# Copying two heads' pairs out of PSUM: both copies on ScalarE in place of one on ScalarE and one on VectorE

## The chip, the core and the metric

The kernel runs on one core of a Trainium2 chip. The core has a matrix engine (TensorE, PE in the profile, with its weight loads listed apart as PEld), two engines for elementwise work (VectorE, DVE; ScalarE, ACT), GpSimd (POOL), and a queue on SyncE (SP) that issues the DMA transfers. TensorE writes into PSUM, which VectorE and ScalarE read. The metric is the device time of one execution in microseconds.

## The reference

Attention with a sigmoid in place of the softmax, and behind it a channel mix with a shift by one token. Batch 8, 12 heads, 448 tokens, head size 64; model size 768, hidden size 1024.

```python
scores = scale * np.matmul(q, k.transpose(0, 1, 3, 2)) - np.log(S)
attn = 1.0 / (1.0 + np.exp(-scores))
x = np.matmul(attn, v)                     # heads side by side: (8, 448, 768)

x_prev = np.concatenate([zeros, x[:, :-1, :]], axis=1)
xk = mu_k * x + (1.0 - mu_k) * x_prev
xr = mu_r * x + (1.0 - mu_r) * x_prev
k = np.maximum(xk @ w_k, 0.0)
v = k * k @ w_v
r = 1.0 / (1.0 + np.exp(-(xr @ w_r)))
return r * v
```

## The kernel before, in words

**Attention.** Two heads make a pair; there are N = 48 pairs, and pair n lies with its two heads on partitions 0 to 63 and 64 to 127. The 448 keys of a head are three chunks of 128 (NC = 3) and a tail of 64. The loop (L415) takes two pairs, n and n + 1, per cycle: 24 cycles. TensorE goes through three ways of tiling its array in a cycle:

- `scores` (L324, matmuls L335): six chunks of scores, three for each pair, in tiles of 64 rows by 128 columns. Each chunk is six matmuls (three products of split operands `kh`, `kl`, `qh`, `ql` for two heads) into a buffer `sc[u]` of two PSUM banks. There are four such buffers; after the first cycle the six chunks use u = 1, 2, 3, 0, 1, 2. Behind each chunk ScalarE computes its sigmoid into `pf` (L359), which frees the buffer.
- `weigh` (L362, matmuls L366): six chunks of sigmoids times values, in tiles of 128 by 64, into `av[0]` for the even pair and `av[1]` for the odd one.
- `score_tails` (L340, L344) for the next two pairs and then `weigh_tails` (L369, L374) for these two, in tiles of 64 by 64. The sigmoid of the score tails goes into `pt`.

`av[0]` and `av[1]` are the two banks of the fourth score buffer, `sc[3]` (L197 to L199). So the third chunk of scores of the next cycle (u = 3; the profile lists its matmuls as L335 with output `av`) can start only when both sums have been copied out, and the first `weigh` only when the sigmoid of that chunk has read it.

**Gather.** `gather(n)` (L380) copies `av[n % 2]` into `xx[n % 2]` (the copy is made by `copy_on`, so it stands under L216 in the profile), subtracts the sum shifted by one token (`dx`, L386), and makes two mixes on VectorE, `mr` and `mk` (L389), which SP's queue stores to `xr_d` and `xk_d`. In the kernel before, the copy of an even pair is on ScalarE and that of an odd pair on VectorE.

**What else runs meanwhile.** The weights come in a 64-bit format and VectorE converts them to 32 bits during attention (`convert`, L226); seven combinations of each group of blocks are made for a product scheme with seven multiplications, and those of the router weight `w_r` are split by a cast on ScalarE and a subtraction on VectorE into `slot` (L291, L292). The next pairs' q and k are split in `prepare` (L308): the casts of even pairs on ScalarE, of odd pairs on VectorE.

**The channel mix.** Three stages (R_, K_, V_) of products of 128 by 128 by 448, `multiply` (L564, matmuls L575), each with its operands fetched and split by ScalarE and VectorE.

**The order of the work.** Each operation is entered with `op(engine, cost, prio, ...)`. `Plan.order` (L50) simulates the engines with these costs: a free engine takes, of the operations that are ready, the one with the smallest due time (prio), and a result is ready for another engine 170 ns after its end (WAIT). The program is written in the order of these starts, and each engine then works through its own list in that order; waits come from the tiles that operations share. TensorE's operations are kept in the order in which they are entered. Costs in ns around the change: sigmoid 923, a chunk of scores 591 (plus 184 at the change of tiling), `weigh_tails` 752, the copy on ScalarE `act(S)` = 474, on VectorE `dve(S)` = 602. Due times in cycle n: `prepare` n + 1, `weigh_tails` n + 1.5, the score tails of the next pairs n + 1.7, both gathers n + 1.8, the next cycle's score chunks and sigmoids n + 2 to n + 2.5. The conversions of the weights have due times by a pace of their own.

Of the kernel before, what the change touches and what calls it, by code (L numbers as in the profile page):

```python
# [22 lines left out]
class Plan:  # L23
# [8 lines left out]
    def op(self, engine, cost, prio, run, reads, writes, dma=None):  # L32
        i = len(self.ops)
        deps = set()
        for r in reads:
            if r in self.writer:
                deps.add(self.writer[r])
        for w in writes:
            if w in self.writer:
                deps.add(self.writer[w])  # L40
            deps.update(self.readers.get(w, ()))
        for r in reads:
            self.readers.setdefault(r, []).append(i)
        for w in writes:
            self.writer[w] = i
            self.readers[w] = []
        deps.discard(i)
        self.ops.append(Op(engine, cost, prio, run, deps, dma))
# [50 lines left out]
def attention_then_channel_mix(  # L99
# [15 lines left out]
    nc = tc.nc  # L115
    P = 128
    N, _, S = q.shape
# [81 lines left out]
    av = [sc[3][:, m] for m in range(2)]  # L199

    plan = Plan()
    op = plan.op
    SP, PE, ACT, DVE = "SP", "PE", "ACT", "DVE"
# [5 lines left out]
    def act(n, sbuf=False, ptr=False):  # L209
        return 100 + 0.834 * n + 42 * sbuf + 93 * ptr  # L210

    def dve(n, fast=False, ptr=False):
        return 135 + n / (1.92 if fast else 0.96) + 61 * ptr

    def copy_on(e, dst, src):
        (nc.scalar.copy if e == ACT else nc.vector.tensor_copy)(dst, src)  # L216
# [4 lines left out]
    def dma(dst, src, prio, reads, writes):  # L221
        ns = dst.shape[0] * math.prod(dst.shape[1:]) * 4 / 300
        op(SP, 500, prio, lambda: nc.sync.dma_start(dst, src), reads, writes, dma=ns)  # L223
# [94 lines left out]
    AV = [("sc", 3, h) for h in range(2)]  # L318
# [61 lines left out]
    def gather(n, at):  # L380
        b, j = divmod(n, NP)
        x, d, X, G = xx[n % 2], dx[0], ("xx", n % 2), ("dx", 0)
        cols = slice(b * S, (b + 1) * S)
        e = DVE if n % 2 else ACT
        op(e, act(S) if e == ACT else dve(S), at, lambda: copy_on(e, x[:, 1:], av[n % 2][:, :S]), [AV[n % 2]], [X])
        op(DVE, dve(S), at, lambda: nc.vector.tensor_sub(d, x[:, 1:], x[:, :S]), [X], [G])  # L386
        for name, m, mu, to, stage in (("mr", mr[n % 2], mur, xr_d, R_), ("mk", mk[n % 2], muk, xk_d, K_)):
            M = (name, n % 2)
            op(DVE, dve(S, ptr=True), at, lambda m=m, mu=mu: nc.vector.scalar_tensor_tensor(m, d, mu[:, j:j + 1], x[:, :S], ALU.mult, ALU.add), [X, G, (mu is muk, "mu")], [M])  # L389
            dma(to[j][:, cols], m, at, [M], [("x", stage, j, b)])  # L390
# [24 lines left out]
    for n in range(0, N, 2):  # L415
        early = FILL * (n < 4)
        if n == 0:
            for c, u in enumerate((1, 2, 3)):
                key_chunk(0, c, u, 0)
            prepare(1, -4)  # L420
            last_keys(0, 0.1)
            for c, u in enumerate((1, 2, 0)):
                key_chunk(1, c, u, 0.2)
        else:
            for i, u in enumerate((1, 2, 3, 0, 1, 2)):
                key_chunk(n + i // NC, i % NC, u, n + 0.1 * i)
        for m in (n + 2, n + 3):
            if m < N:
                if m > 2:
                    load(m, n + 0.2 - early)  # L430
                prepare(m, n + 1 - early)
        for m in (n, n + 1):
            for c in range(NC):
                weigh(m, c, n + 1)
        if n + 2 < N:
            last_keys(n + 2, n + 1.7)
        weigh_tails(n, n + 1.5)
        gather(n, n + 1.8)
        gather(n + 1, n + 1.8)
# [19 lines left out]
    e = N % RAW  # L459
# [173 lines left out]
    for stage, w, out7, pace in ((K_, w_k, wk_o, WK_PACE), (V_, w_v, wv_o, WV_PACE)):  # L633
        at = OFF + first[stage - 1]
# [5 lines left out]
    for step, (stage, s, p) in enumerate(steps):  # L640
        at = OFF + step
# [53 lines left out]
```

## Time and profile before

| | before |
|---|---|
| median of 3 runs | 819.69 us (819.4 to 820.19) |
| profiled execution | 818.95 us, of which the span from first to last instruction is 817.2 us |
| granted TensorE clock | 1.000 |
| TensorE matmuls busy | 809.1 us (99%) |
| VectorE busy | 631.5 us (77%) |
| ScalarE busy | 486.9 us (60%) |
| end of attention's last matmuls | 258.3 us from the span's start |

A line of a timeline reads: start in us, duration in us, engine, line, operation, output <- inputs, shapes, count, and in brackets how long the engine stood idle before it and what ended that. In a list of waits the three numbers are microseconds in total, number of times and the longest. In a list of groups they are the busy time in us, the mean in ns of one, and behind the bar the idle time of the engine just before them with what ended it. In the chain in order of time a line reads: start, duration, what. Busy shares are averages over attention and channel mix, which have different limits.

### The profile page before, as it was taken

The page shows a single profiled execution, that of the slowest core. Times are in us where ns is not written, and L with a number is a line of the kernel's source. Part 1 is how long each engine was busy: PE and PEld are TensorE (multiplying, and loading weights), DVE is VectorE, ACT ScalarE, POOL GpSimd, SP SyncE. Part 2 cuts the span into 40 slices and gives each one's busy share as a digit, 9 for nine tenths or more (in the row PEclk, how much of TensorE's full clock was granted, in tenths as well). Part 3 has the DMA queues.
Part 4 walks back from the last instruction along what each step waited for, and adds up shares of the span by engine and source line. Part 5 has one row for each costly group of instructions (what it writes and reads, how often), then busy time and mean ns, then how long its engine had stood idle before and what let it go on. Part 6 is the DMA issues. An engine that isn't in the chain of part 4 may idle for free.

```text
span 817.2 us, 13460 instructions
## 1 busy us (share of the span) xinstructions
PE 809.1 (99%) x4594; PEld 648.8 (79%) x4594; DVE 631.5 (77%) x1184; ACT 486.9 (60%) x833; POOL 0.3 (0%) x6
## 2 busy tenths in 40 slices
PE   8999999999999999999999999999999999999998
PEld 3445455555556999999999999999999999999997
DVE  4989988888889898989898937347497584775944
ACT  5676777777766555556676555656775334343341
POOL 0000000000000000000000000000000000000000
PEclk9999999999999999999999999999999999999999
DMA  7877788788886879576887663523775546655415
GB/s 244 280 238 253 254 253 257 249 277 269 285 290 236 309 226 340 176 274 226 310 241 277 234 205 124 157 92 124 226 224 187 173 155 218 204 180 157 156 47 168
DMA packets 104756, 179.69 MB, mean 220 GB/s; under 512 B 11888, under 2 KB 93296, under 8 KB 104688
## 3 DMA queue, kind: packets, MB, share of 16 engines
q1 hardware_dynamic: 104688, 178.83, 66.5%
q8 instruction: 36, 0.59, 0.3%
q14 instruction: 32, 0.26, 0.1%
HBM read 109.06 MB, written 69.73 MB: 219 GB/s over the span
## 4 chain that ended last, share of the span: by engine, by line
PE 99%; DMA 0%; ACT 0%; issue 0%; DVE 0%; SPq 0%; ACTq 0%
PE pb L575 68%; PE av L366 14%; PE sc L335 10%; PE sc L344 3%; PE av L335 3%; PE av L374 2%; DMA qn<-in_q 0%; PE pb L562 0%; ACT pf L359 0%; DVE pt L606 0%; ACT kh L216 0%; ACT qh L216 0%; SPq L223 0%; ACTq L216 0%
## 5 line engine op out<-in xcount | busy, mean ns | idle before, releaser
L575 PE MATMUL pb<-rr,slot 128*128 128x448 f32 x2076 | 437.1, 362 | 0.0
L575 PEld LDWEIGHTS pb<-rr,slot 128*128 128x128 f32 x2076 | 389.2, 187 | 26.0
L575 PE MATMUL pb<-qh,slot 128*128 128x448 f32 x464 | 151.9, 361 | 0.0
L366 PE MATMUL av<-pf,vn 128*64 128x448 f32 x576 | 113.5, 543 | 0.6 <-ACT pf L359 0.6
L359 ACT ACTIVATE pf<-sc 128x896 f32<-128x896 f32 x120 | 103.6, 940 | 5.5 <-PE sc L335 5.5
L575 PEld LDWEIGHTS pb<-qh,slot 128*128 128x128 f32 x464 | 86.9, 187 | 6.5
L366 PEld LDWEIGHTS av<-pf,vn 128*64 128x64 f32 x576 | 39.2, 137 | 63.7 <-issue 52.9
L575 PE MATMUL pb<-ql,slot 128*128 128x448 f32 x232 | 84.2, 363 | 0.0
L510 ACT CAST rr<-ys 128x448 fp32r<-128x448 f32 x66 | 36.3, 567 | 45.9 <-PE pb L575 45.1
L359 ACT ACTIVATE pt<-sc 128x896 f32<-128x896 f32 x24 | 22.0, 918 | 58.3 <-PE sc L344 58.3
L511 DVE TENSOR_TENSOR rr<-ys,rr 128x448 fp32r<-128x448 f32 x66 | 39.0, 618 | 9.7 <-ACT rr L510 9.6
L335 PE MATMUL sc<-qh,kh 64*128 64x448 f32 x236 | 46.1, 387 | 0.0
L575 PEld LDWEIGHTS pb<-ql,slot 128*128 128x128 f32 x232 | 43.5, 188 | 2.2
L511 DVE TENSOR_TENSOR rr<-pf,rr 128x448 fp32r<-128x448 f32 x38 | 23.2, 623 | 26.4 <-ACT rr L510 26.4
L335 PE MATMUL sc<-ql,kh 64*128 64x448 f32 x236 | 43.0, 361 | 0.0
L335 PE MATMUL sc<-qh,kl 64*128 64x448 f32 x236 | 42.8, 359 | 0.0
L613 ACT COPY pb<-pb 128x448 f32<-128x448 f32 x40 | 20.7, 518 | 32.9 <-PE pb L575 32.9
L617 ACT COPY pf<-pb 128x448 f32<-128x448 f32 x40 | 21.3, 532 | 31.7 <-PE pb L575 28.4
L510 ACT CAST rr<-vn 128x448 fp32r<-128x448 f32 x50 | 27.9, 564 | 19.0 <-PE pb L575 17.6
L335 PEld LDWEIGHTS sc<-qh,kh 64*128 64x128 f32 x236 | 22.1, 184 | 20.1 <-issue 16.9
L511 DVE TENSOR_TENSOR rr<-vn,rr 128x448 fp32r<-128x448 f32 x50 | 29.7, 621 | 6.5 <-ACT rr L510 6.5
L511 DVE TENSOR_TENSOR rr<-qn,rr 128x448 fp32r<-128x448 f32 x28 | 17.4, 621 | 21.7 <-ACT rr L510 21.7
(110 smaller groups left out, 1035.6 us busy)
## 6 DMA issues: line engine op xcount, KB each, us to landing
kn<-in_k SPq DMA_DIRECT2D x48, 224.0 KB, 4.3
qn<-in_q SPq DMA_DIRECT2D x48, 224.0 KB, 4.4
vn<-in_v SPq DMA_DIRECT2D x48, 224.0 KB, 4.5
xr_d<-mr SPq DMA_DIRECT2D x48, 224.0 KB, 4.5
xk_d<-mk SPq DMA_DIRECT2D x48, 224.0 KB, 4.5
pf<-r_d SPq DMA_DIRECT2D x48, 224.0 KB, 3.2
k_d<-pf SPq DMA_DIRECT2D x34, 224.0 KB, 2.1
r_d<-pf SPq DMA_DIRECT2D x28, 224.0 KB, 3.4
```

What stands on the lines that cost most here:

```text
L335: nc.tensor.matmul(sc[u][:, h, :S], kk[half[h], c * P:(c + 1) * P], qq[half[h], :], start=e == 0, stop=e == len(pairs) - 1)
L344: nc.tensor.matmul(sc[u][half[h ^ (m % 2)], m % 2, :S], kn[m % RAW][half[h], KW:], qn[m % RAW][half[h], :], start=True, stop=True)
L359: op(ACT, 923, at, lambda: nc.scalar.activation(f, sc[u][:, :, :S], AF.Sigmoid, bias=NEG_LOG_S, scale=SCALE), R, K)
L366: nc.tensor.matmul(av[n % 2][half[h], :S], vn[n % 5][:, h * NC + c, :], pf[i][:, h, :], start=c == 0, stop=False)
L374: nc.tensor.matmul(av[m % 2][half[r ^ (m % 2)], :S], vn[m % 5][half[r], 2 * NC, :], pt[n // 2 % PTB][half[r], m % 2, :], start=False, stop ...
L510: op(ACT, act(T, True), at, lambda: nc.scalar.copy(hi, y), [Y], [H])
L511: op(DVE, dve(T), at, lambda: nc.vector.tensor_sub(lo, y, hi), [Y, H], [L])
L575: nc.tensor.matmul(b[0], l, r, start=p in (0, 4) and (t, e) == (0, 0), stop=(t, e) == (n - 1, 2), skip_group_check=True)
L613: op(ACT, act(T), at, lambda: nc.scalar.copy(y(), x()), [X], [Y])
L617: op(ACT, act(T), at, lambda: nc.scalar.copy(u, y()), [Y], [U])
```

## The change

Both gathers copy on ScalarE, with the cost `act(S)` in the planner. The copy is now `nc.scalar.copy` in `gather` itself. Since the planner orders the whole program from costs and due times, the order of other operations may differ too.

```diff
         x, d, X, G = xx[n % 2], dx[0], ("xx", n % 2), ("dx", 0)
         cols = slice(b * S, (b + 1) * S)
-        e = DVE if n % 2 else ACT
-        op(e, act(S) if e == ACT else dve(S), at, lambda: copy_on(e, x[:, 1:], av[n % 2][:, :S]), [AV[n % 2]], [X])
+        op(ACT, act(S), at, lambda: nc.scalar.copy(x[:, 1:], av[n % 2][:, :S]), [AV[n % 2]], [X])
         op(DVE, dve(S), at, lambda: nc.vector.tensor_sub(d, x[:, 1:], x[:, :S]), [X], [G])
```

## Prediction

> **What bounds the kernel now.** I read the page first: its busy times and the chain that ended last.
>
> ```profile
> PE 809.1 (99%) x4594; PEld 648.8 (79%) x4594; DVE 631.5 (77%) x1184; ACT 486.9 (60%) x833; POOL 0.3 (0%) x6
> ...
> PE 99%; DMA 0%; ACT 0%; issue 0%; DVE 0%; SPq 0%; ACTq 0%
> PE pb L575 68%; PE av L366 14%; PE sc L335 10%; PE sc L344 3%; PE av L335 3%; PE av L374 2%; DMA qn<-in_q 0%; PE pb L562 0%; ACT pf L359 0%; DVE pt L606 0%; ACT kh L216 0%; ACT qh L216 0%; SPq L223 0%; ACTq L216 0%
> ```
>
> The chain is TensorE from end to end, so a copy out of PSUM matters only where a matmul waits for it. A busy PE hides such waits, because the end of a matmul is modelled; they show at the weight load in front of it. So the next view is the waits, first those of the weight loads between 10 and 258 us, then those of all engines between 20 and 350 us.
>
> ```profile
> PEld av L335 <- DVE xx L216: 4.3, 12, 0.4
> PEld av L335 <- ACT xx L216: 3.9, 11, 0.4
> ```
>
> ```profile
> DVE xx L216 <- ACT xx L216: 13.3, 12, 1.5
> ...
> ACT xx L216 <- DVE xx L216: 6.7, 11, 1.2
> ```
>
> The third score chunk of a cycle is computed into the bank pair `av` (L335 with output av). It waits 12 + 11 = 23 times, once in every cycle that has a successor, 0.36 us each (8.2/23), for whichever copy into `xx` comes second. And the copies do not run side by side, as the planner believes: in 12 cycles VectorE's waits for ScalarE's, in 11 ScalarE's for VectorE's. They take turns. The timeline of one cycle where VectorE goes first:
>
> ```profile
> 154.10 0.93 PE L374 MATMUL av<-pt,vn 64*64 64x448 f32 x8
> ...
> 154.37 0.92 ACT L359 ACTIVATE pt<-sc 128x896 f32<-128x896 f32 x1 [1.44 <-PE sc L344]
> ...
> 155.12 0.62 DVE L216 COPY xx<-av 128x448 f32<-128x448 f32 x1 [0.97 <-PE av L374]
> ...
> 155.84 0.54 ACT L216 COPY xx<-av 128x448 f32<-128x448 f32 x1 [0.55 <-DVE xx L216]
> ...
> 156.07 0.37 PE L335 MATMUL sc<-ql,kh 64*128 64x448 f32 x2
> 156.27 1.73 ACT L359 ACTIVATE pf<-sc 128x896 f32<-128x896 f32 x2
> ...
> 156.42 0.19 PEld L335 LDWEIGHTS av<-qh,kh 64*128 64x128 f32 x2 [0.36 <-ACT xx L216]
> 156.42 0.47 PE L335 MATMUL av<-qh,kh 64*128 64x448 f32 x2
> ...
> 156.73 0.37 PE L335 MATMUL av<-qh,kl 64*128 64x448 f32 x2
> ...
> 157.87 0.94 ACT L359 ACTIVATE pf<-av 128x896 f32<-128x896 f32 x1
> ...
> 158.14 0.19 PEld L335 LDWEIGHTS sc<-qh,kh 64*128 64x128 f32 x2
> ```
>
> The weighted sums end at 155.03 (154.10 + 0.93). VectorE copies until 155.74, ScalarE from 155.84 to 156.38, and TensorE may go on at 156.42. Without a wait, pairs of matmuls follow each other every 0.20 us: 156.07, 156.27, 156.47. The second pair of the waiting chunk starts at 156.73 instead of 156.47, so the wait costs **0.26 us** per cycle, not the 0.36 that the weight load stands idle; the rest is its head start. This 0.26 is the most that any faster copying can win.
>
> The other kind of cycle, ScalarE first, from the timelines of ScalarE, VectorE and the weight loads:
>
> ```profile
> 102.11 0.92 ACT L359 ACTIVATE pt<-sc 128x896 f32<-128x896 f32 x1 [1.69 <-PE sc L344]
> 102.93 0.53 ACT L216 COPY xx<-av 128x448 f32<-128x448 f32 x1
> 103.62 1.73 ACT L359 ACTIVATE pf<-sc 128x896 f32<-128x896 f32 x2 [0.17 <-PE sc L335]
> ```
>
> ```profile
> 103.49 0.62 DVE L216 COPY xx<-av 128x448 f32<-128x448 f32 x1 [1.21 <-ACT xx L216]
> ```
>
> ```profile
> 104.17 0.18 PEld L335 LDWEIGHTS av<-qh,kh 64*128 64x128 f32 x2 [0.36 <-DVE xx L216]
> ```
>
> **The main term: the two copies.** Removed are VectorE's 24 copies and the hand-over between the engines; added are 24 copies on ScalarE.
>
> ```profile
> L216 DVE COPY xx<-av 128x448 f32<-128x448 f32 x24 | 15.0, 626 | 24.0 <-ACT xx L216 13.3 <-PE av L374 10.7
> ...
> L216 ACT COPY xx<-av 128x448 f32<-128x448 f32 x24 | 12.8, 533 | 7.2 <-DVE xx L216 7.2
> ```
>
> When can ScalarE begin? It is busy with the sigmoid of the tails (`pt`). In the second cycle a copy follows that sigmoid's start by 0.82 us (102.11 to 102.93). In the first cycle that is 154.37 + 0.82 = 155.19, a little behind the 155.12 at which VectorE could begin, so the first copy starts 0.07 later than today. How far behind it does the second start? Two copies in a row are nowhere in the trace. The nearest row is a copy followed by another read of PSUM on ScalarE: 155.84 to 156.27, 0.43. The lower bound is 0.41 (a copy followed by a cast out of SBUF, in cycles that carry one), the upper bound 0.54, the copy's whole duration, if two copies do not overlap at all. I take 0.43, the case nearest in operation and memory. Second copy: 155.62 to 156.16, weight load at 156.20 with today's 0.04, second matmul pair 0.31 behind it as today, at 156.51 instead of 156.73: **0.22 us** won of the 0.26. In the other kind of cycle 102.11 + 0.82 + 0.43 + 0.53 + 0.04 = 103.93 against 104.17, 0.24. I take 0.22 for all: 23 x 0.22 = **5.1 us**. With the bounds of the pitch: 0.41 gives 0.24 and 5.5, 0.54 gives 0.11 and 2.5.
>
> [...]
>
> [...]
>
> **The second term: what stands between the copies and the next sigmoid.** Four cycles lose time at another place as well. The chain in order of time, a long cycle and a normal one, and the other three long ones:
>
> ```profile
> 16.54 0.91 PE sc L344 x8
> ...
> 27.58 0.91 PE sc L344 x8
> ...
> 41.91 2.04 PE sc L335 x18
> ...
> 83.77 2.04 PE sc L335 x18
> ...
> 94.40 2.04 PE sc L335 x18
> ...
> 111.51 0.91 PE sc L344 x8
> ...
> 115.45 2.04 PE sc L335 x18
> ...
> 122.15 0.91 PE sc L344 x8
> ...
> 142.96 0.91 PE sc L344 x8
> ...
> 146.90 1.80 PE sc L335 x18
> ...
> 153.36 0.91 PE sc L344 x8
> ```
>
> A normal cycle is 153.36 - 142.96 = 10.40 us, the long one 10.64; its last three chunks take 2.04 instead of 1.80. ScalarE's and the weight loads' timelines say why:
>
> ```profile
> 113.98 0.54 ACT L216 COPY xx<-av 128x448 f32<-128x448 f32 x1 [0.55 <-DVE xx L216]
> 114.41 0.52 ACT L291 CAST slot<-wbits 128x384 fp32r<-128x384 f32 x1
> 114.82 1.73 ACT L359 ACTIVATE pf<-sc 128x896 f32<-128x896 f32 x2
> ```
>
> ```profile
> 116.61 0.18 PEld L335 LDWEIGHTS sc<-qh,kh 64*128 64x128 f32 x2 [0.31 <-ACT pf L359]
> ```
>
> A cast of router weights (0.41 to the next start) sits between copy and sigmoids; the sixth chunk needs the bank that the second sigmoid frees, and waits. The planner put the cast there because it had a hole: counting from the end of the score tails it sees ScalarE free at 170 + 923 + 474 = 1567 ns, but the next sigmoid ready only at 752 + 591 + 184 + 170 = 1697. With a second copy of 474 ScalarE is taken until 2041, the sigmoid is ready by then, and it is due earlier (n + 2) than these casts, which run ahead of their due times. So the cast moves behind the sigmoids, where ScalarE has room (1.44 us idle before `pt` above). 4 x 0.24 = **1.0 us**. If the casts stay, 0; below that the same hole costs 0.24 in cycles that now escape it, which I put into the no-change rival. The first cycle, 27.58 - 16.54 = 11.04, has 0.64 over the normal one; whether the new order mends that I cannot tell, so it goes only into the low end.
>
> **What costs nothing, and why.** The first sigmoid starts behind both copies. In the first cycle above it keeps its 0.43 to the second copy and comes 0.22 earlier with everything behind it; where ScalarE goes first today it comes at 102.93 + 0.86 = 103.79 instead of 103.62. Cover: two sigmoids from 155.62 + 0.43 end at 157.78, and the weight load of the sixth chunk, 158.14 today, would come at 157.92. That leaves 0.14, less 0.04 of signalling 0.10. This is the tightest cover; gone, it costs the 0.24 of the long cycles. VectorE loses 24 copies of 626 ns, which frees nothing that TensorE waits for. Its subtractions now wait for ScalarE's second copy, at 156.16 where today the later copy ends at 156.38 in this cycle; the mixes and SP's stores behind them move the same way. The channel mix has no matmul waiting for these copies, so it starts earlier by the sum and keeps its length.
>
> **Sum.** 5.1 + 1.0 = 6.1 us off the profiled execution's own 818.95 (a span of 817.2 and 1.75 around it): 812.85. The median of the runs is 819.69, 0.74 above that execution: **813.6**.
>
> **The rivals.**
> 1. *The copies do not overlap on ScalarE* (pitch 0.54): 2.5 + 1.0 = 3.5, 816.2. For it: no row of two such copies in a row. Against it: every pair of ScalarE instructions above without a wait between starts before the first has ended (102.11 + 0.92 is 103.03, the copy starts at 102.93).
> 2. *The wait moves to the sixth chunk.* If the first sigmoid is late by more than the cover of 0.10, by a slower pair of copies or by casts that stay behind them, each cycle pays 0.24 there and gains 0.22 before: 23 x 0.02 = 0.5 lost, without the second term, about 820, no change. For it: the cover is thin. Against it: copies and sigmoids shift together, and the order of due times.
> 3. *Casts land in front of the copies* (slower). ScalarE takes its queue in order; a cast between the sigmoid of the tails and the copies delays both by 0.41, so a cycle loses 0.41 - 0.22 = 0.19: in all 23, 4.4 lost, 824. It turns slower than today where the mean delay exceeds 0.22 a cycle. For it: the casts of q and k are due at n + 1, ahead of the copies at n + 1.8, and ScalarE's run of work is one copy longer. Against it: ScalarE stands idle 1.44 and 1.69 us before `pt` in the two cycles above, room for one more copy of 0.43, and no copy above has a cast in front. [...]
>
> **How the numbers follow.** Forecast 0.72, rival 1 0.10, rival 2 0.10, rival 3 0.08. A measurement of this kernel tells about 0.2% (1.6 us) from no change; forecast and rival 1 are faster by more, rival 2 is within, rival 3 slower: 0.82, 0.10, 0.08. The low end takes the whole 0.26 in all cycles (6.0), the 1.0 and the 0.64: 7.6 off, 812.0. The high end reaches past rival 1 to a gain of about 2.5, the first term's bound alone: 817.2. That leaves out rivals 2 and 3.
>
> **What would show it.** Step one: ScalarE's two copies into `xx` 0.41 to 0.45 apart, and the wait of the weight load for `av` at 0.14 us or less in place of 0.36. Step two: no cast between copies and sigmoids, chain pieces of 1.80 throughout, cycles of about 10.18 us, and an attention that ends some 6 us earlier than today's 258. Rival 2 would show weight loads for `sc` waiting for `pf` about 0.3 us in most cycles; rival 3 a cast between `pt` and `xx`. A channel mix whose length changes by over 0.5 us would make the prediction wrong at a place that I did not look for.

## The result, and the profile after

The changed kernel takes **814.51 us** (median of 6 runs, 813.95 to 814.88) where the kernel before takes 819.71 beside it (819.07 to 820.28): a ratio of 0.9936, 95% interval 0.9923 to 0.9949, so 5.2 us or 0.64% less. 813.6 was forecast.

The page after, busy times and the chain by line (in the changed file, the lines behind the edit have a number one smaller, and the copy stands under L384):

```profile
PE 803.4 (99%) x4594; PEld 649.4 (80%) x4594; DVE 619.5 (76%) x1160; ACT 495.5 (61%) x857; POOL 0.3 (0%) x6
...
PE 98%; ACT 1%; DMA 0%; issue 0%; DVE 0%; SPq 0%
```

VectorE has 24 instructions less, ScalarE 24 more, and the chain is still TensorE's. All copies into `xx`, from the view of that tile, and the waits of the weight loads between 10 and 258 us:

```profile
L384 ACT COPY xx<-av x48: 527/539/556, 18.6 to 253.9; 128x448 f32<-128x448 f32 x48
```

```profile
PEld av L335 <- ACT xx L384: 1.0, 1, 1.0
```

Of 23 waits for a copy, 8.2 us in total, one is left, of 1.0 us. A cycle in the timeline:

```profile
140.33 0.93 PE L374 MATMUL av<-pt,vn 64*64 64x448 f32 x8
...
140.60 0.92 ACT L359 ACTIVATE pt<-sc 128x896 f32<-128x896 f32 x1 [2.27 <-PE sc L344]
...
141.41 0.96 ACT L384 COPY xx<-av 128x448 f32<-128x448 f32 x2
...
142.26 1.75 ACT L359 ACTIVATE pf<-sc 128x896 f32<-128x896 f32 x2
142.30 0.37 PE L335 MATMUL sc<-ql,kh 64*128 64x448 f32 x2
...
142.43 0.19 PEld L335 LDWEIGHTS av<-qh,kh 64*128 64x128 f32 x2
...
142.51 0.40 PE L335 MATMUL av<-qh,kh 64*128 64x448 f32 x2
...
142.74 0.37 PE L335 MATMUL av<-qh,kl 64*128 64x448 f32 x2
```

Both copies together take 0.96, with 0.54 for one: the second starts 0.42 behind the first, and the sigmoids 0.85 behind the first. The second matmul pair of the third chunk starts at 142.74, 0.44 behind the last pair of the second chunk; without any wait it would be 0.40. So 0.04 of the 0.26 us is left. The whole attention, in the chain in order of time:

```profile
16.73 0.98 PE sc L344 x8
...
27.61 0.91 PE sc L344 x8
...
231.21 0.91 PE sc L344 x8
...
241.39 0.96 PE sc L344 x8
...
244.20 0.88 ACT xx L384 x2
...
252.47 0.91 PE av L374 x8
253.38 0.81 PE pb L561 x3
...
281.39 527.43 PE pb L574 x2637
```

For comparison the end of the attention of before in the same view:

```profile
246.96 0.91 PE sc L344 x8
...
257.35 0.91 PE av L374 x8
258.26 0.81 PE pb L562 x3
...
286.26 527.42 PE pb L575 x2637
```

Where the time went, interval by interval: the 21 cycles from the second score tails on take 241.39 - 27.61 = 213.78, 10.18 each, where they took 246.96 - 27.58 = 219.38: **-5.60**. The first interval takes 10.88 in place of 11.04: -0.16. The last takes 11.08 in place of 10.39: **+0.69**. That is -5.07 from the first score tails to the first matmul of the channel mix. The channel mix is as long as before (the stretch of 2637 matmuls takes 527.43 and 527.42). The first score tails come 0.19 later in this execution, as the first matmuls do (4.12 against 3.92). In the profiles below these tails start between 15.8 and 17.1 us, so below I compare the stretch from the first score tails to the channel mix ("the attention": 241.72 us before, 236.65 after, each from one profiled execution) beside the medians.

### The profile page after: what moved, and what is told of

Its sections match the earlier page's. It is cut to its first block, busy times and chain, and to the rows that moved or that the text cites. A ratio compares the mean times of both kernels' runs of the same rounds, so it can differ in the third digit from the quotient of the medians.

```text
span 812.3 us, 13502 instructions
## 1 busy us (share of the span) xinstructions
PE 803.4 (99%) x4594; PEld 649.4 (80%) x4594; DVE 619.5 (76%) x1160; ACT 495.5 (61%) x857; POOL 0.3 (0%) x6
## 4 chain that ended last, share of the span: by engine, by line
PE 98%; ACT 1%; DMA 0%; issue 0%; DVE 0%; SPq 0%
PE pb L574 68%; PE av L366 14%; PE sc L335 9%; PE sc L344 3%; PE av L374 2%; PE av L335 2%; DMA qn<-in_q 0%; ACT xx L384 0%; ACT pt L359 0%; ACT pf L359 0%; PE pb L561 0%; DVE pt L605 0%; ACT rr L509 0%; ACT kh L216 0%; ACT qh L216 0%
## 5 line engine op out<-in xcount | busy, mean ns | idle before, releaser
L385 DVE TENSOR_TENSOR dx<-xx 128x448 f32<-128x448 f32 x48 | 29.8, 621 | 18.2 <-ACT xx L384 18.1
```

## The experiments

| kernel | median us | ratio to before (95%) | attention us |
|---|---|---|---|
| before | 819.2 to 819.7 | | 241.72 |
| the change | 814.51 | 0.9936 (0.9923 to 0.9949) | 236.65 |
| order alone | 819.14 | 0.9998 (0.9989 to 1.0008) | 242.64 |
| engine alone | 816.90 | 0.9971 (0.9959 to 0.9982) | 239.32 |
| filler behind the copies | 822.09 | 1.0040 (1.0025 to 1.0054) | 244.93 |
| filler ahead of the copies | 825.67 | 1.0082 (1.0067 to 1.0097) | 248.73 |
| two tiles, two engines | 812.11 | 0.9915 (0.9901 to 0.9930) | 235.20 |
| two tiles, one engine | 813.39 | 0.9931 (0.9917 to 0.9946) | 236.12 |
| last casts later | 813.00 | 0.9925 (0.9912 to 0.9937) | 235.73 |
| last and first casts later | 812.69 | 0.9921 (0.9908 to 0.9935) | 235.04 |
| two tiles, last and first later | 812.20 | 0.9913 (0.9900 to 0.9927) | 234.86 |

Each ratio is to runs of the kernel before on the same chip. Order alone, engine alone and the two kernels with later casts share one chip; the fillers and the first two kernels with two tiles share another; the last row is from a third.

### Order alone, engine alone

The change does two things: the copy moves, and the planner, which now sees two copies on ScalarE, orders the rest differently. Each was run by itself. The order alone, against the changed kernel:

```diff
-        op(ACT, act(S), at, lambda: nc.scalar.copy(x[:, 1:], av[n % 2][:, :S]), [AV[n % 2]], [X])
+        op(ACT, act(S), at, lambda: copy_on(DVE if n % 2 else ACT, x[:, 1:], av[n % 2][:, :S]), [AV[n % 2]], [X])
```

> The changed kernel's plan (both copies entered as ScalarE's), but the odd pair's copy is issued on VectorE as before. Theory (two separable terms): the long cycles go (1.0 us), the copies still take turns (0.26 us in each of 23 cycles stays), the casts in the last cycle cost their share: about 819.0 to 819.6, the waits for xx about 0.36 us, 23 times. Rival (the order of the work is what brought the gain): about 815.

819.14, no change, and inside the theory's range. The waits of the weight loads, and the timeline of the one cycle that was not expected:

```profile
PEld av L335 <- DVE xx L216: 10.5, 23, 1.5
```

```profile
28.43 0.36 DVE L235 TENSOR_SCALAR wbits<-wraw 128x384 uint32<-128x384 uint32 x1 [1.18 <-DMA wraw<-in_moe_w_r]
...
29.61 0.53 ACT L216 COPY xx<-av 128x448 f32<-128x448 f32 x1
...
31.32 0.62 DVE L216 COPY xx<-av 128x448 f32<-128x448 f32 x1
...
31.99 0.18 PEld L335 LDWEIGHTS av<-qh,kh 64*128 64x128 f32 x2 [1.51 <-DVE xx L216]
```

All 23 waits are back, and the 20 cycles from the third score tails on take 10.40 each: the long ones are gone by order alone, as expected. In the profiled execution what it wins is lost again, by the casts of the last cycle (11.48 in place of 10.39) and by 1.1 us in the cycle shown: VectorE's copy stands in its queue behind a row of conversions that had waited 1.18 us for the transfer of a weight. That execution took 820.72 us, 1.6 more than the median, so its attention, 0.92 longer than before, need not be typical. With both copies on ScalarE none stands behind VectorE's conversions.

The engine alone, against the kernel before:

```diff
-        op(e, act(S) if e == ACT else dve(S), at, lambda: copy_on(e, x[:, 1:], av[n % 2][:, :S]), [AV[n % 2]], [X])
+        op(e, act(S) if e == ACT else dve(S), at, lambda: nc.scalar.copy(x[:, 1:], av[n % 2][:, :S]), [AV[n % 2]], [X])
```

> The plan of the kernel before (costs, engines and so the order), but both copies are issued on ScalarE. Theory: 23 x 0.22 = 5.1 us off, the last cycle keeps its order and loses nothing, the casts between copies and sigmoids stay: 0.24 us in the 4 cycles that pay today and in up to 4 that had cover when VectorE copied second: 814.6 to 815.6. Rival (order): about 819.

816.90, above the theory's range: 2.4 us less attention (in a profiled execution of 815.86) in place of the 4.1 to 5.1. Waits of the weight loads, and ScalarE's timeline in one cycle:

```profile
PEld sc L335 <- ACT pf L359: 2.1, 7, 0.3
```

```profile
203.24 0.53 ACT L385 COPY xx<-av 128x448 f32<-128x448 f32 x1
203.93 0.92 ACT L359 ACTIVATE pf<-sc 128x896 f32<-128x896 f32 x1 [0.16 <-PE sc L335]
204.75 0.53 ACT L385 COPY xx<-av 128x448 f32<-128x448 f32 x1
```

Seven cycles wait for a sigmoid behind a cast, 4 as before and 3 that had cover as long as VectorE copied second: 0.7 us. The rest I had not thought of. In this cycle the plan, which believes the second copy to be VectorE's and late, puts it behind a sigmoid; the third chunk waits, and the interval is 11.25 in place of 10.18. Near the end two more intervals, of 10.64 and 10.63, hold casts for the channel mix in the wrong place: in front of a sigmoid, and between the two copies. So the engine alone wins 5.1 and loses 2.7, the order alone wins nothing, and only both together win 5.1 (in the medians 2.3, 0.1 and 5.2). The theory had two separable terms; they are not independent. A planner must know on which engine an operation runs.

### Fillers

Two copies of a spare tile of 128 columns, without planned cost, on ScalarE behind the second copy of each cycle, or in front of the first:

```diff
+        def go():
+            parts = [lambda: nc.scalar.copy(x[:, 1:], av[n % 2][:, :S])]
+            if n % 2 == 1:                      # ahead: n % 2 == 0 and parts[0:0]
+                parts[1:1] = [lambda: nc.scalar.copy(spare_, spare_)] * 2
+            for part in parts:
+                part()
+
-        op(ACT, act(S), at, lambda: nc.scalar.copy(x[:, 1:], av[n % 2][:, :S]), [AV[n % 2]], [X])
+        op(ACT, act(S), at, go, [AV[n % 2]], [X])
```

> The changed kernel with a filler of about 0.4 us on ScalarE (two copies of a spare tile of 128 columns, no planned cost) behind the two copies of every cycle, so in front of the first sigmoid. Theory: the sixth chunk has a cover of about 0.10 us, the rest costs about 0.24 us as in the long cycles of before: 23 x 0.24 = 5.5, 820.0, and weight loads for sc that wait for pf in every cycle. Rival (ScalarE has room there, the long cycles had another cause): 814.5.

> The changed kernel with the same filler of about 0.4 us in front of the two copies. Theory: since the third chunk has at most some hundredths of a us left, the whole filler is paid in each cycle: 23 x 0.4 = 9.2, about 823.7. If a filler ahead cost no more than one behind (about 820), the cover of the third chunk would be larger than I read it.

822.09 and 825.67, each about 2 us above the number of its theory. With the filler behind the copies, the waits of the weight loads, ScalarE's timeline, and the weight load that pays:

```profile
PEld sc L337 <- ACT pf L361: 12.5, 46, 0.3
```

```profile
145.36 0.97 ACT L387 COPY xx<-av 128x448 f32<-128x448 f32 x2
146.20 0.65 ACT L389 COPY spare<-spare 128x128 f32<-128x128 f32 x2
146.76 1.72 ACT L361 ACTIVATE pf<-sc 128x896 f32<-128x896 f32 x2
```

```profile
148.53 0.19 PEld L337 LDWEIGHTS sc<-qh,kh 64*128 64x128 f32 x2 [0.30 <-ACT pf L361]
```

The weight loads for `sc` wait for a sigmoid 46 times, two for each of 23 cycles, where the changed kernel has no such wait: this is as the theory said, and the rival is out. The filler is longer than meant, 0.56 us (146.20 to 146.76). The attention is 8.28 longer than after the change, 0.36 a cycle: 0.56 less a cover (a delay that no matmul feels) of **0.20**. A cast of 0.41 costs 0.24 by the long cycles of before, which gives 0.17. My 0.10 was the cover of the weight load; here a weight load can be some 0.1 late before a matmul is (0.20 less 0.10; before the change 0.36 idle less 0.26 lost). With the filler ahead:

```profile
147.07 0.62 ACT L389 COPY spare<-spare 128x128 f32<-128x128 f32 x2
147.60 0.96 ACT L387 COPY xx<-av 128x448 f32<-128x448 f32 x2
```

```profile
148.62 0.19 PEld L337 LDWEIGHTS av<-qh,kh 64*128 64x128 f32 x2 [0.67 <-ACT xx L387]
```

Here the filler takes 0.53 (147.07 to 147.60) and the attention is 12.08 longer, 0.53 a cycle: ahead of the copies nothing is covered any more. Both prices bear out the mechanism; the numbers of the theories were too low because they took the filler for 0.4, the author's estimate, which no run had shown.

### Why the copies take turns

The prediction read from the waits that the two copies take turns. If it is the program that orders them, over the one tile whose halves both read, then two tiles should set them free (the sigmoid of that chunk becomes two instructions of 448 columns):

```diff
-    sc += ring(pav, "av", 1, [P, 2, 512], F32)
-    av = [sc[3][:, m] for m in range(2)]
+    av = ring(pav, "av", 2, [P, 512], F32)
+
+    def bank(u, h):
+        return av[h][:, :S] if u == 3 else sc[u][:, h, :S]
```

> The kernel before, with the two banks of av made two tiles instead of the halves of one; the sigmoid of the third chunk is then two instructions of 448 columns. The copies stay on two engines. Theory (it is the shared tile, by the program, that makes the copies take turns): now both run from about 0.1 us after the weighted sums, no wait for xx is left, the cycle is 10.15 to 10.25 us: 813 to 815. Rival (the turn-taking is not the program's tile): the waits of 0.36 us stay, 819.5 to 821 with the split sigmoid.

> The changed kernel with the same two tiles for av: the control for the run with two tiles and two engines. Both theories: ScalarE takes the copies one behind the other anyway, so 814.5, plus what the split sigmoid costs, 0 to 1.5 us (it has about 0.1 us of cover in a cycle).

812.11 and 813.39, both below what was expected (813 to 815, and 814.5 to 816). The two copies in the timeline of two tiles on two engines:

```profile
140.81 0.62 DVE L218 COPY xx<-av 128x448 f32<-128x448 f32 x1 [0.84 <-PE av L383]
140.87 0.53 ACT L218 COPY xx<-av 128x448 f32<-128x448 f32 x1
...
141.76 0.19 PEld L337 LDWEIGHTS av<-qh,kh 64*128 64x128 f32 x2
...
141.96 0.36 PE L337 MATMUL av<-qh,kh 64*128 64x448 f32 x2
```

They run side by side and neither is slower for it (0.62 and 0.53), the third chunk starts 0.20 behind the pair before it, and the normal cycle is 10.14 us. So the turn-taking was the shared tile's, and VectorE's copy was not the trouble in itself.

Whether two engines then beat one is less clear. On the same chip it is 812.11 against the control's 813.39, and in the attention 235.20 against 236.12. But the control's cycles are 10.17 to 10.18, as after the change, only 0.03 to 0.04 longer, and the whole difference of 0.92 lies in the last interval. The chain there with two engines, then with one:

```profile
240.81 0.91 PE sc L346 x8
...
250.95 0.91 PE av L383 x8
```

```profile
239.91 0.91 PE sc L346 x8
...
250.99 0.91 PE av L383 x8
```

It takes 10.14 and 11.08, because the control has the casts of the next section in front of its copies. Up to there the two take 224.15 and 224.13: what two engines win in the first interval and in the normal cycles they lose again in two longer ones (10.68 and 10.53). Against the changed kernel itself two tiles on two engines have 1.45 us less attention and a median 2.4 us lower, but these medians were not taken side by side, and the intervals of the two ratios overlap.

### What the change lost in the last cycle, and what stays to be won

ScalarE's timeline of the changed kernel where the one wait is left:

```profile
242.37 0.92 ACT L359 ACTIVATE pt<-sc 128x896 f32<-128x896 f32 x1 [1.37 <-PE sc L344]
243.18 1.02 ACT L509 CAST rr<-ys 128x448 fp32r<-128x448 f32 x2
244.10 0.97 ACT L384 COPY xx<-av 128x448 f32<-128x448 f32 x2
```

Two casts for the first operands of the channel mix, due at N - 4 = 44 and so ahead of the copies due at 45.8, delay these by 0.92 us (243.18 to 244.10): the weighted sums end at 243.05 (L374, 242.12 and 0.93), and ScalarE goes through its list in the order written. Due later, against the changed kernel:

```diff
-    right(R_, 0, 0, N - 4)
+    right(R_, 0, 0, N - 1.4)
```

> The changed kernel, with one due time more changed: the first three operands of the channel mix are due behind the last pairs' sigmoids (N - 1.4) instead of at N - 4. Theory: in the last cycle two casts into rr stand between the sigmoid of the tails and the two copies, and the third chunk of scores waits about 1.0 us there, 0.9 us more than in the other cycles; moved, this goes: about 0.9 us under the changed kernel, 813.6, and no wait of the av weight load for xx over 0.15 us. Rival: the casts only move the wait to the start of the channel mix, which then begins later: 814.5, no change.

813.00, where 813.6 was expected; the firmer number is the attention, 0.92 shorter, as the theory said. No weight load for `av` waits for `xx` any more, and the channel mix is as long as after the change (555.4 us from its first matmul to its last in both), which rules out the rival. The last two intervals in the chain are 10.17 each:

```profile
230.49 0.91 PE sc L344 x8
...
240.66 0.91 PE sc L344 x8
...
250.83 0.91 PE av L374 x8
```

The first interval has two casts of q and k between sigmoids, due early in the second pass of the loop:

```diff
-                prepare(m, n + 1 - early)
+                prepare(m, n + 1 - FILL * (n < 2))
```

> As the run with the later casts, and the early due time of the q and k casts is taken away in the second pass of the loop, where two casts stand between the second and the third sigmoid of the first long stretch. Theory: the first interval between score tails, 10.88 us, falls to 10.2: another 0.7 us, 812.9. Rival: the casts are then late for the next cycle's scores, 813.6 or more.

812.69: the attention is another 0.69 shorter, the first interval 10.18, but the median falls by only 0.3. The chain in the channel mix shows a new wait:

```profile
251.98 27.01 PE pb L574 x135
...
279.02 0.62 DVE kn L620
279.64 0.21 DVE wbits L238
...
280.02 0.63 DVE rr L510
...
280.70 526.29 PE pb L574 x2630
```

An operand is split on VectorE behind a conversion, and TensorE waits until 280.70, 1.7 us behind the end of the stretch before. From its first matmul to its last the channel mix takes 555.8 us in place of 555.4, and these 0.4 are what the median lacks of the 0.7. Both due times with the two tiles:

> The two tiles for av with the copies on two engines, in the order of before, and both due times moved as in the runs on the last and the first cycle. Theory: the gains add up, since they lie in different cycles; the interval before the last but one score tails falls from 10.54 to 10.14 and the first from 10.34 to 10.14 or so: 0.6 us under the 812.1 of the two tiles alone, 811.5, the shortest of all. Rival: the early casts were already behind cover there and the later casts push the start of the channel mix: 812.1 or more.

812.20, the rival's number: the attention is 0.34 shorter than with the tiles alone. Both intervals fall as the theory said (the first from 10.34 to 10.14, the one before the last score tails from 10.53 to 10.13), but one cycle in the middle takes 10.94, and the gains don't add up. In that cycle VectorE's list has the subtraction for the even pair, which waits for ScalarE's copy, ahead of VectorE's own copy (the one wait of a weight load for `av` on a copy of VectorE is 0.7 us long); that is not the cause that the rival named. The two tiles alone (812.11) and this kernel cannot be told apart.

## Why the prediction was right, and where it was off

**The main term, 0.22 us a cycle, came out in the normal cycles**: 10.18 where 10.40 stood. Each part of it is in the trace: the copy starts 0.81 to 0.82 behind the sigmoid of the tails, the second 0.42 behind the first where 0.43 was taken, the remaining loss is the forecast 0.04. Rival 1, no overlap, is ruled out by the 0.96 for two copies.

**The second term, 4 x 0.24, came too**: there is no long cycle among the 21, and 21 x 0.22 + 4 x 0.24 = 5.58 against the measured 5.60. The run of the order alone has none either, so it is the planner's doing. What the prediction did not say is that the two terms hold only together: with the engine moved under the old order, 2.7 of 5.1 us are lost.

**The step that failed is the sum over all 23 cycles with nothing lost elsewhere.** Rival 3, a cast in front of the copies, was given as one mechanism for all cycles, and was looked for only among the casts of q, k and the router weights. It struck in one: the casts for the channel mix, due ahead of the copies, enter the queue in the last cycle. In place of a gain of 0.22 that interval lost 0.69. With 0.16 for the first interval instead of its 0.22, this makes the 5.07 measured in place of 6.1, and in the medians 5.2. Moving the due time gave 0.92 back, which is the whole of it.

**Rival 2's cover** was read 0.10 us; the filler measures 0.20, so the forecast was safer from that rival than it claimed to be.

**That the copies take turns** was read rightly, and the two tiles show that it is the program that orders them. The prediction drew only half of the conclusion: that the change removes the hand-over. The other half is that the order itself could go: that wins the whole 0.26 in a normal cycle (10.14) and needs no move between the engines.

## What to carry to other kernels

When two engines share a job "in parallel", look in the timeline whether they do: here each waited for the other over a tile whose halves both read, and that order, not the split itself, cost 0.26 us a cycle. Price a wait at the start of the matmuls, not at the idle weight load (0.36 idle were 0.26 lost), and after moving work onto an engine go through every kind of instruction that can enter its queue ahead of it, in the first and last cycles too. A planner's order is part of an edit: changing engine and plan together took 5.2 us off the median, the engine without the plan 2.3, and the plan without the engine made no difference.

## What the runs showed of the hardware that was not expected

In the cycle shown of two tiles on two engines, ScalarE and VectorE read the two tiles of `av` in PSUM at the same time, and neither copy is slower for it: 0.53 and 0.62 us side by side, 533 and 626 ns in turns in the kernel before. And a copy of only 128 columns within SBUF still takes ScalarE 0.27 to 0.28 us from start to start (two in 0.53 to 0.56), where 448 columns out of PSUM take 0.42: this filler is dearer than its columns suggest. Its second copy writes what the first one wrote, and whether that order is part of the price was not tried.
